# A retention layer and a SoLU block on one core: another written order of every engine's steps, with the loads of q, k and v placed one by one

## The chip, the cores and the metric

The kernel runs on one core of a Trainium2 chip. The metric is the device time of one execution in microseconds (us), as the median of several runs. The engines are called as the profile calls them: PE is TensorE (PEld its weight loads), DVE is VectorE, ACT is ScalarE, POOL is GpSimd, and SP is SyncE, whose queue issues nearly all DMA transfers.

## What is computed

```
# q, k, v: (8 batches, 8 heads, 576 tokens, 64), float32
scores = (q @ k.T) / 8
ret    = scores * gamma_h ** (row - col)   # 0 above the diagonal
x      = (ret @ v), heads side by side     # (4608 tokens, 512)
h      = x @ w_in                          # (4608, 1024)
solu   = h * softmax(h)
ln     = (solu - mean) / sqrt(var + 1e-6) * g_ln
out    = ln @ w_out                        # (4608, 512), float32
```

## The kernel before

The 4608 tokens are cut into 36 chunks of 128. Batches go in pairs: chunks 0, 2, 4, 6 are the first four pieces of batch 0, chunks 1, 3, 5, 7 those of batch 1, and chunk 8 holds the last 64 tokens of both; then the next pair begins. Retention is done in chunked form: within a chunk as masked scores times v, from earlier chunks through a state of 64 x 64 a head that each chunk passes on.

Nothing is scheduled by a tool. The string ORDER lists some 950 steps, `name:chunk:options`, and `run` (L826) calls them one after the other. Each engine gets its instructions in the order in which they are written there, and works them off in that order; between engines only semaphores order the work. So an instruction that waits holds up all that stands behind it on its engine. The steps of a chunk are:

- `ld` (L265): three transfers, q, k and v of the chunk, 256 KB each, on SP's queue. `li` (L778) loads one of four blocks of 128 rows of w_in, `lo` (L787) two of the eight blocks of w_out; each is 512 KB.
- `cq`, `ck`, `cv` (L285, L298, L310): q, k and v are scaled and cast to 16 bits, on POOL (`:g`), DVE (`:v`) or ACT (`:a`).
- `tq` and `eq` (L313, L363): PE transposes q and k (32 matmuls of 128 columns), and an engine copies the result to SBUF. In its place stand for some late chunks `tr`, `er` (L335, L344: q alone) and `kd` (L322: a DMA transpose of k).
- `sc` (L374) and `mk` (L387): the scores on PE, and two products with the mask on DVE.
- `kv` (L397), `ad` (L411), `dk` (L425), `d3` (L438): k.T v on PE, its addition to the state on DVE, and two decayed copies of the state on POOL.
- `av` (L449), `fs` (L463), `ex` (L482): x on PE from the scores and from the state; its cast to 16 bits.
- `m1` (L498): h, 16 matmuls of 512 columns. Chunks 0 and 1 do it with `mr` (L487), one row block of w_in at a time, each as soon as `wi` (L782) has cast it.
- `mx` (L508), `xp` (L515), `so` (L523): the row maximum on DVE, the exponential on ACT, the product h times exp on DVE, called u. h has two buffers in PSUM (`ps_h`, tag h): the matmuls of a chunk may begin when `so` of the chunk that held the buffer has ended.
- `ce` (L535): for the first five chunks (PLAIN = 5) the mean is taken from u, by two DVE instructions. For later ones the mean lies in w_out: `mm` (L809) multiplies w_out by ones, `mc` (L816) and `ws` (L820) subtract the mean from w_out.
- `sq` (L548), `ra` (L561), `rp` (L578): the sum of squares on ACT, two instructions on 128 x 1 on POOL or DVE, and their power on POOL.
- `tu` and `eu` (L584, L597), or `du` (L592): u transposed by PE (16 matmuls of 128 columns) and copied, or by a DMA transpose.
- `wo` (L792): a block of w_out is scaled and cast. `m2` (L602): the output product, 16 matmuls of 512 columns. `st` (L612): scaling on ACT, and the transfer to HBM.
- `wu` (L735): matmuls on zeros, which fill PE while it waits. The last chunk, 35, is done in halves of 512 columns (`hm` to `hw`, L628 to L717).

The strings BANKS and SLOTS say which PSUM bank and which buffer of a ring each tile takes. RINGS gives the depth of the rings, and is the same in both kernels.

## Time and profile before

| | |
|---|---|
| time, median of 3 runs | 211.8 us (211.57 to 212.08) |
| span of the profiled execution, first to last instruction | 210.9 us |
| PE, PEld busy | 92%, 59% |
| DVE, ACT, POOL busy | 86%, 81%, 75% |
| DMA moved | 47.71 MB, 226 GB/s on the mean |

The profile shows one execution. It has its span and no time of its own; the median of the runs stands 0.9 us above that span. In the rows of the trace the first number is the start in us from the span's start, the second the length; in brackets stands how long the engine was idle before, and what ended the idle time. In the rows by stage each engine has its busy time in the stage, and the number of its instructions.

### The profile page before, as it was taken

What the parts mean: (1) busy time and instruction counts of PE and PEld (TensorE: products, weight loads), DVE (VectorE), ACT (ScalarE), POOL (GpSimd) and SP (SyncE); (2) the same over time, 40 slices, a digit from 0 to 9 for tenths busy, and PEclk for the clock granted to TensorE, in tenths of its full rate; (3) what the DMA queues carried; (4) which work ended last, traced back from release to release, by engine and by line L of the source; (5) the groups of instructions that cost most, each with busy time, mean ns of one, the idle gap of its engine ahead of it and who ended that gap; (6) DMA issues with size and microseconds to landing.
All of it is one profiled execution on the core that took longest, in us unless ns stands there. A gap on an engine that the chain in (4) does not pass through costs nothing.

```text
span 210.9 us, 7583 instructions
## 1 busy us (share of the span) xinstructions
PE 194.3 (92%) x3125; PEld 124.0 (59%) x3125; DVE 181.4 (86%) x323; ACT 170.5 (81%) x299; POOL 157.2 (75%) x226
## 2 busy tenths in 40 slices
PE   0887798999999999999999999999999998999992
PEld 0464476575666657657566667575656654565562
DVE  0486999979997999899989999999879998999760
ACT  2424999898979999999898978999679976677981
POOL 5377899676689899888839798879999977545620
PEclk9999999999999999999999999999999999999999
DMA  5999998999898989999999899999989999899754
GB/s 134 257 330 294 258 272 290 253 209 299 224 215 258 265 215 273 221 251 230 208 275 197 205 231 238 273 226 206 179 143 256 210 166 205 156 247 199 154 174 149
DMA packets 110834, 47.71 MB, mean 226 GB/s; under 512 B 94536, under 2 KB 104784, under 8 KB 110800
## 3 DMA queue, kind: packets, MB, share of 16 engines
q1 hardware_dynamic: 110480, 47.07, 99.7%
q8 instruction: 24, 0.39, 0.8%
q10 hardware_dynamic: 320, 0.16, 0.3%
...
## 4 chain that ended last, share of the span: by engine, by line
PE 55%; SPq 14%; DMA 8%; DVE 8%; POOL 7%; ACT 3%; issue 3%; DVEq 0%; POOLq 0%
PE o L256 21%; PE h L256 18%; SPq L274 5%; SPq L270 5%; DMA w_out<-in_moe_w_out_dram 3%; PE tp L251 3%; PE sc L381 3%; PE lp L251 3%; DMA qkT<-k 2%; PE x L456 2%; POOL v L279 2%; SPq L789 2%; DMA qf<-in_q_dram 2%; PE x L256 2%; SPq L779 2%
## 5 line engine op out<-in xcount | busy, mean ns | idle before, releaser
L256 PE MATMUL h<-w_in,xT 128*64 128x512 f16 x560 | 66.9, 380 | 0.1
L256 PE MATMUL o<-w_c,uT 128*64 128x512 f16 x480 | 56.9, 380 | 0.0
L394 DVE TENSOR_TENSOR ret<-sc,tris 128x512 f16<-128x512 f32 x72 | 46.1, 682 | 2.8 <-PE sc L381 2.5
L256 PEld LDWEIGHTS <-xT 128*64 128x64 f16 x576 | 31.5, 110 | 23.1 <-issue 0.7
L512 DVE TENSOR_REDUCE nm<-h 128x1 f32<-128x1024 f32 x35 | 42.6, 1216 | 2.8 <-PE h L256 2.7
L256 PEld LDWEIGHTS <-uT 128*64 128x64 f16 x560 | 31.0, 110 | 23.0 <-issue 0.6
L527 DVE SCALAR_TENSOR_TENSOR u<-h,e 128x1024 f16<-128x1024 f32 x35 | 42.5, 1215 | 1.5 <-ACT e L518 1.4
L518 ACT ACTIVATE e<-h,nm 128x1024 f32<-128x1024 f32 x35 | 39.4, 1125 | 5.0 <-DVE nm L512 3.1
L432 POOL TENSOR_TENSOR s<-t,small 128x512 f16<-128x512 f32 x32 | 33.9, 1063 | 7.4 <-DVE t L420 6.1
L555 ACT ACTIVATE sq<-u,su 128x1024 bf16<-128x1024 f16 x30 | 34.8, 1159 | 2.0 <-DVE u L527 2.0
L581 POOL TENSOR_TENSOR rs<-w,mhalf 128x1 f32<-128x1 f32 x36 | 20.3, 570 | 20.7 <-DVE w L572 17.2
L290 POOL TENSOR_TENSOR q<-qf,small 128x512 f16<-128x512 f32 x30 | 31.2, 1043 | 5.4 <-DMA qf<-in_q_dram 5.1
L279 POOL TENSOR_TENSOR v<-vf,small 128x512 f16<-128x512 f32 x30 | 31.7, 1062 | 2.8 <-DMA vf<-in_v_dram 2.5
L615 ACT ACTIVATE o_sb<-o,rs 128x512 f32<-128x512 f32 x35 | 24.0, 692 | 4.5 <-POOL rs L581 3.2
L243 ACT COPY qkT<-tp 128x512 f16<-128x512 f16 x42 | 23.0, 599 | 5.0 <-PE tp L251 4.9
L243 ACT CAST xT<-x 128x512 f16<-128x512 f32 x29 | 17.1, 593 | 3.1 <-PE x L256 2.8
L251 PE MATMUL tp<-ident,q 128*64 128x128 f16 x232 | 12.4, 230 | 6.0 <-POOL q L290 5.5
L243 ACT CAST k<-kf 128x512 f16<-128x512 f32 x17 | 10.5, 626 | 7.7 <-DMA kf<-in_k_dram 7.7
L456 PE MATMUL x<-ret,v 128*64 128x128 f16 x288 | 14.8, 222 | 2.1 <-DVE ret L394 1.5
L251 PEld LDWEIGHTS <-q 128*64 128x64 f16 x280 | 11.0, 115 | 8.9 <-POOL q L290 5.7
L381 PE MATMUL sc<-qkT 64*128 64x128 f16 x288 | 14.7, 223 | 1.3 <-DMA qkT<-k 0.8
L444 POOL TENSOR_TENSOR s<-t,small 128x256 f32<-128x256 f32 x24 | 15.3, 638 | 0.9 <-DVE t L420 0.8
...
## 6 DMA issues: line engine op xcount, KB each, us to landing
...
uT<-u SPq DMA_TRANSPOSE x16, 4.6
...
```

The source lines that it names most:

```text
L243: (engine.copy if engine is nc.scalar else engine.tensor_copy)(out=out, in_=in_)
L251: nc.tensor.transpose(out=out[w], in_=in_[:, w], identity=ident)
L256: nc.tensor.matmul(out=out[w], lhsT=lhsT[:, w], rhs=rhs, start=start, stop=stop, skip_group_check=True,)
L279: engine.tensor_tensor(out=dst, in0=T.pop((key, n)), in1=table.unsqueeze(2).to_broadcast([P, H, D]), op=ALU.mult,)
L290: ENG[e].tensor_tensor(out=dst.rearrange("p (a h) d -> p h a d", h=2), in0=T.pop(("qf", n)).rearrange("p (h a) d -> p h a d", h=2), in1=ta ...
L394: nc.vector.tensor_tensor(out=r, in0=s, in1=m, op=ALU.mult)
L432: nc.gpsimd.tensor_tensor(out=s16, in0=t.unsqueeze(2).to_broadcast([P, 4, 2, D]), in1=gd.unsqueeze(3).to_broadcast([P, 4, 2, D]), op=ALU.mult,
L512: nc.vector.tensor_reduce(out=nm, in_=T["h", n], axis=AX.X, op=ALU.max, negate=True)
L518: nc.scalar.activation(out=e, in_=T["h", n], func=ACT.Exp, bias=T.pop(("nm", n)), accum_out=s)
L527: nc.vector.scalar_tensor_tensor(out=u, in0=T.pop(("h", n)), scalar=-1.0, in1=T.pop(("e", n)), op0=ALU.mult, op1=ALU.mult, accum_out=su,)
L555: nc.scalar.activation(out=s, in_=T.pop(("v", n)), func=ACT.Square, scale=-float(DFF), bias=T.pop(("su", n)), accum_out=ss,)
L615: nc.scalar.activation(out=o_sb, in_=T.pop(("o", n)), func=ACT.Copy, scale=T.pop(("rs", n)))
```

## The change

ORDER, BANKS and SLOTS are written anew. `ld` is taken apart into `lq`, `lk` and `lv`, so that each of the three transfers of a chunk has its own place in the order. The helper `both` makes the transposed tile of q and k where the first of its two halves needs it. The rules BY_DMA and BY_PE, which turned `tr`, `er` and `kd` of some chunks into `tq`, `eq` or nothing, are gone: the order names the step itself.

What the engines do in all stays nearly the same. PE has 32 transposes of u fewer (17 chunks by `tu`, 18 by `du`; 19 and 16 before) and 8 matmuls on zeros fewer (12, before 20). Of the pairs of `ra` 30 are on POOL (19 before) and 6 on DVE (17). `cv` is on DVE ten times (six), on POOL 26 times (30); `wo` is on POOL five times (three). SP issues two DMA transposes more. All else is a matter of order.

```diff
-BY_DMA = 12
-BY_PE = (12, 13, 14, 15, 16, 18, 19, 20, 21, 22, 23, 24, 25, 27)
 ORDER = """
-c1:0 ld:1 ld:0 cq:1:g cv:1:v ck:1:a cq:0:g tq:1 eq:1:av wu:2:2 wu:5:2 ck:0:a cv:0:g sc:1 ld:2 mk:1
...
+c1:0 lv:1 li:3 lk:1 lq:2 lq:1 ck:1:a lk:2 cv:1:v lq:0 wu:4:1 lq:4 cq:2:g gt:0 lk:0 li:0 ck:2:a
...
-    def ld(n):
-
-        for key, src in (("qf", q), ("kf", k), ("vf", v)):
-            dst = ring(load, [P, H, D], FP, key)
...
-            T[key, n] = dst
+    def load_one(n, key, src):
+        dst = ring(load, [P, H, D], FP, key)
+        if key == "qf" and quads(n) or key == "kf" and chunks[n][1] == 4:
+            nc.sync.dma_start(
+                out=dst.rearrange("p (h a) d -> p h (a d)", h=2), in_=fours(src, n)
+            )
+        else:
+            nc.sync.dma_start(out=dst, in_=tokens(src, n))
+        T[key, n] = dst
+
+    def lq(n):
+        load_one(n, "qf", q)
+
+    def lk(n):
+        load_one(n, "kf", k)
+
+    def lv(n):
+        load_one(n, "vf", v)
...
+    def both(n):
+
+        if ("qkT", n) not in T:
+            T["qkT", n] = ring(att, [P, 2, 4, P], F16, "qkT")
+        return T["qkT", n]
+
     def kd(n):
-        if chunks[n][1] == 4 or n < BY_DMA or n in BY_PE:
-            return
-        T["qkT", n] = ring(att, [P, 2, 4, P], F16, "qkT")
+
         nc.sync.dma_start_transpose(
-            out=T["qkT", n][:, 1], in_=T["k16", n].rearrange("p h d -> p (h d)")
+            out=both(n)[:, 1], in_=T["k16", n].rearrange("p h d -> p (h d)")
         )
...
     def tr(n):
-        if chunks[n][1] == 4 or n < BY_DMA or n in BY_PE:
-            return tq(n)
+
         tp = bank([P, 4, P], F16, "tr")
...
     def er(n, e="a"):
-        if chunks[n][1] == 4 or n < BY_DMA or n in BY_PE:
-            return eq(n, e)
-        turned(ENG[e], n, T["qkT", n][:, 0], T.pop(("tp", n)))
+        turned(ENG[e], n, both(n)[:, 0], T.pop(("tp", n)))
```

Three places show how the engines' orders differ. The first is the start of SP's queue. Before, q, k and v of chunk 1 are its first three transfers; the rows show what follows (qf, kf and vf are the loads of q, k and v: of chunk 0, of chunk 2, then the four blocks of w_in, then chunk 4).

```order
L270 DMA qf_118<-in_q_dram 128x2x256
L274 DMA kf_120<-in_k_dram 128x8x64
L274 DMA vf_122<-in_v_dram 128x8x64
L270 DMA qf_176<-in_q_dram 128x2x256
L274 DMA kf_178<-in_k_dram 128x8x64
L274 DMA vf_180<-in_v_dram 128x8x64
L779 DMA w_in32_94<-in_moe_w_in_dram 128x1024 x4
L270 DMA qf_371<-in_q_dram 128x2x256
L274 DMA kf_373<-in_k_dram 128x8x64
L274 DMA vf_375<-in_v_dram 128x8x64
```

SP's queue now, from its ninth transfer on (k of chunk 0, block 0 of w_in, v of 0, block 2, k of 4, block 1, v of 4, v of 2). Ahead of these rows stand v of 1, block 3 of w_in, k of 1, q of 2, q of 1, k of 2, q of 0 and q of 4.

```order
L275 DMA kf_138<-in_k_dram 128x8x64
L790 DMA w_in32_94<-in_moe_w_in_dram 128x1024
L275 DMA vf_176<-in_v_dram 128x8x64
L790 DMA w_in32_94<-in_moe_w_in_dram 128x1024
L275 DMA kf_196<-in_k_dram 128x8x64
L790 DMA w_in32_94<-in_moe_w_in_dram 128x1024
L275 DMA vf_212<-in_v_dram 128x8x64
L275 DMA vf_221<-in_v_dram 128x8x64
```

The last block of w_in was the 13th transfer, behind nine loads; it is the 14th now, behind ten, though the first block has moved up to the second place. v of chunk 4 was the 16th transfer and is the 15th, and v of chunk 2 was the ninth and is the 16th.

The second place is DVE's queue where the first h are done. Before (h_364 is that of chunk 1, h_379 of chunk 0, h_511 of chunk 2; nm is the maximum, u the product with the exponential):

```order
L512 TENSOR_REDUCE nm_405<-h_364 128x1
L512 TENSOR_REDUCE nm_420<-h_379 128x1
L527 SCALAR_TENSOR_TENSOR u_445,su_446<-h_364,e_415 128x1024
L420 TENSOR_TENSOR t_457<-kp_448,s32_362 128x256
L538 TENSOR_SCALAR nmu_462<-su_446 128x1
L543 TENSOR_SCALAR u_445<-u_445,nmu_462 128x1024
L394 TENSOR_TENSOR ret0_475<-sc0_465,tris_86 128x512
L394 TENSOR_TENSOR ret1_477<-sc1_466,tris_86 128x512
L527 SCALAR_TENSOR_TENSOR u_531,su_532<-h_379,e_508 128x1024
L420 TENSOR_TENSOR t_607<-kp_534,s32_384 128x256
L512 TENSOR_REDUCE nm_627<-h_511 128x1
```

And now (h_299 is that of chunk 1, h_398 of chunk 0, h_523 of chunk 2; t_428 is the state after chunk 2, ret0_450 and ret1_452 are the masked scores of chunk 4). Right ahead of these rows stands the cast of v of chunk 4 (`v16_391<-vf_212`, L289).

```order
L523 TENSOR_REDUCE nm_393<-h_299 128x1
L431 TENSOR_TENSOR t_428<-kp_416,s32_361 128x256
L405 TENSOR_TENSOR ret0_450<-sc0_434,tris_86 128x512
L405 TENSOR_TENSOR ret1_452<-sc1_435,tris_86 128x512
L538 SCALAR_TENSOR_TENSOR u_484,su_485<-h_299,e_395 128x1024
L431 TENSOR_TENSOR t_489<-kp_407,s32_430 128x256
L549 TENSOR_SCALAR nmu_513<-su_485 128x1
L554 TENSOR_SCALAR u_484<-u_484,nmu_513 128x1024
L523 TENSOR_REDUCE nm_542<-h_398 128x1
L523 TENSOR_REDUCE nm_575<-h_523 128x1
L431 TENSOR_TENSOR t_590<-kp_579,s32_426 128x256
L538 SCALAR_TENSOR_TENSOR u_609,su_610<-h_398,e_592 128x1024
```

A cast of v stands ahead of the first maximum; the state of chunk 2 and the masked scores of chunk 4 have moved ahead of the first u; and the maximum of chunk 2 has moved ahead of the u of chunk 0.

The third place is POOL's queue where w_out is cast. Before (w_out16 is the cast block, s32 a decayed state, rs the power of `rp`, w1 and w2 the two of `ra`):

```order
L279 TENSOR_TENSOR v16_766<-vf_656,small_85 128x512
L444 TENSOR_TENSOR s32_771<-t_457,small_85 128x256
L804 TENSOR_TENSOR w_out16_97<-w_out32_95,g32_93 128x512
L444 TENSOR_TENSOR s32_823<-t_607,small_85 128x256
L804 TENSOR_TENSOR w_out16_97<-w_out32_95,g32_93 128x512
L581 TENSOR_TENSOR rs_884<-w2_620,mhalf_88 128x1
L804 TENSOR_TENSOR w_out16_97<-w_out32_95,g32_93 128x512
```

Now:

```order
L443 TENSOR_TENSOR s16_588<-t_489,small_85 128x512
L443 TENSOR_TENSOR s16_595<-t_174,small_85 128x512
L455 TENSOR_TENSOR s32_597<-t_590,small_85 128x256
L443 TENSOR_TENSOR s16_599<-t_590,small_85 128x512
L289 TENSOR_TENSOR v16_622<-vf_278,small_85 128x512
L815 TENSOR_TENSOR w_out16_97<-w_out32_95,g32_93 128x512 x5
L577 TENSOR_SCALAR w1_685<-s_396 128x1
```

Three casts with other work between them have become five in a row, behind the states of chunks 3 and 4 and the v of chunk 6.

177 lines of the change are left out of this document (88 added, 89 removed).

## The prediction

> **What bounds the kernel now.** I read the page's busy shares first, then the busy time by stage, then the timeline of the first 45 us, in which the order has changed most.
>
> ```profile
> span 210.9 us, 7583 instructions
> ...
> PE 194.3 (92%) x3125; PEld 124.0 (59%) x3125; DVE 181.4 (86%) x323; ACT 170.5 (81%) x299; POOL 157.2 (75%) x226
> ```
>
> ```profile
> core 0: us, PE busy (x) PEld busy (x) DVE busy (x) ACT busy (x) POOL busy (x), PEclk, DMA share, GB/s
> 0.00:25.00 25.00, 15.71 (x221) 10.10 (x223) 14.09 (x28) 10.83 (x18) 16.01 (x28) 1.00 1.00 255
> 25.00:30.00 5.00, 5.00 (x100) 3.42 (x100) 4.96 (x10) 4.33 (x10) 4.58 (x7) 1.00 1.07 271
> 30.00:40.00 10.00, 9.32 (x175) 6.38 (x171) 9.79 (x18) 8.80 (x15) 9.61 (x12) 1.00 1.01 274
> ...
> 60.00:80.00 20.00, 20.00 (x350) 12.72 (x348) 17.94 (x31) 18.27 (x32) 18.39 (x26) 1.00 0.95 241
> 100.00:120.00 20.00, 19.52 (x308) 12.04 (x306) 18.46 (x33) 17.75 (x31) 14.28 (x20) 1.00 1.01 223
> 140.00:160.00 20.00, 19.24 (x322) 12.36 (x317) 18.23 (x31) 16.57 (x32) 18.25 (x28) 1.00 1.02 195
> 160.00:180.00 20.00, 19.18 (x310) 11.64 (x308) 18.41 (x33) 16.58 (x30) 17.09 (x23) 1.00 1.16 202
> ```
>
> Two regimes are to be seen. From 60 us on PE is busy in 20.00 of 20.00 us, or lacks 0.48 (100 to 120), 0.76 (140 to 160) and 0.82 (160 to 180), 2.1 us in all: there the end comes when PE's work is through, and a step moved costs something only if PE waits for it. In the first 25 us PE works 15.7, and between 25 and 40 us it is DVE that is full, 4.96 of 5 and 9.79 of 10, with POOL at 9.61 of 10. There the transfers set when work can begin, and DVE's queue sets how fast it goes on. PE cannot make up later what it loses there, since later it is full. So the time after is the time before, plus what the head loses, minus the work that PE no longer has, plus or minus the waits in the middle.
>
> **The pace of the transfers.** Instructions that waited for a transfer tell when it landed; here the first, the ninth, the 13th (the last block of w_in) and the 16th of SP's queue.
>
> ```profile
> 4.41 1.04 POOL L290 TENSOR_TENSOR q<-qf,small 128x512 f16<-128x512 f32 x1 [1.21 <-DMA qf<-in_q_dram]
> ...
> 13.52 1.04 POOL L279 TENSOR_TENSOR v<-vf,small 128x512 f16<-128x512 f32 x1 [0.29 <-DMA vf<-in_v_dram]
> ...
> 19.27 0.43 DVE L243 CAST w_in<-w_in 128x512 f16<-128x512 f32 x1 [0.98 <-DMA w_in<-in_moe_w_in_dram]
> ...
> 22.22 1.04 POOL L279 TENSOR_TENSOR v<-vf,small 128x512 f16<-128x512 f32 x1 [0.45 <-DMA vf<-in_v_dram]
> ```
>
> Eight loads took 9.11 us, 1.14 each; four blocks of w_in 5.75, 1.44 each; the next three loads 2.95, 0.98 each. With 1.14 and 1.44 the last block of w_in, now the 14th transfer behind nine loads and three blocks after the first, lands at 4.41 + 9 x 1.14 + 4 x 1.44 = 20.4 (before 19.27), v of chunk 4 at 21.6, v of chunk 2 at 22.7. With 0.98 a load all three come 1.4 to 1.8 us sooner. The early block of w_in gains nothing by itself: h of chunk 1 needs all four.
>
> **Term 1, DVE's chain in the head.** These rows show the chain before.
>
> ```profile
> 20.66 2.52 DVE L512 TENSOR_REDUCE nm<-h 128x1 f32<-128x1024 f32 x2 [0.96 <-PE h L256]
> ...
> 23.16 1.23 DVE L527 SCALAR_TENSOR_TENSOR u<-h,e 128x1024 f16<-128x1024 f32 x1
> ...
> 23.31 0.32 PE L405 MATMUL kp<-v,k 128*64 128x64 f16 x8 [0.95 <-POOL v L279]
> ...
> 24.20 0.61 POOL L243 CAST k<-kf 128x512 f16<-128x512 f32 x1
> ...
> 25.11 1.89 PE L256 MATMUL h<-w_in,xT 128*64 128x512 f16 x16
> ...
> 25.22 1.28 DVE L394 TENSOR_TENSOR ret<-sc,tris 128x512 f16<-128x512 f32 x2
> ...
> 26.42 1.21 DVE L527 SCALAR_TENSOR_TENSOR u<-h,e 128x1024 f16<-128x1024 f32 x1
> ...
> 28.73 1.49 PE L256 MATMUL h<-w_in,xT 128*64 128x512 f16 x12
> ```
>
> ```profile
> 37.40 1.92 PE L256 MATMUL h<-w_in,xT 128*64 128x512 f16 x16
> ...
> 38.60 1.03 POOL L804 TENSOR_TENSOR w_out<-w_out,g 128x512 f16<-128x512 f32 x1
> ...
> 40.52 3.21 PE L256 MATMUL o<-w_out,uT 128*64 128x512 f16 x28 [0.32 <-ACT w_out L797]
> ...
> 48.73 0.41 PE L251 MATMUL tp<-ident,k 128*64 128x128 f16 x8 [0.42 <-DVE k L243]
> ```
>
> ```profile
> L432 POOL TENSOR_TENSOR s<-t,small 128x512 f16<-128x512 f32 x32 | 33.9, 1063 | 7.4 <-DVE t L420 6.1 <-DVE t L418 0.9
> L279 POOL TENSOR_TENSOR v<-vf,small 128x512 f16<-128x512 f32 x30 | 31.7, 1062 | 2.8 <-DMA vf<-in_v_dram 2.5
> ...
> L420 DVE TENSOR_TENSOR t<-kp,s 128x256 f32<-128x256 f32 x24 | 10.0, 419 | 2.0 <-PE kp L405 1.3 <-POOL s L444 0.5
> ...
> L243 DVE COPY qkT<-tp 128x512 f16<-128x512 f16 x16 | 8.7, 567 | 0.4 <-ACT qkT L243 0.3
> ...
> L279 DVE TENSOR_TENSOR v<-vf,small 128x512 f16<-128x512 f32 x6 | 4.1, 690 | 6.1 <-DMA vf<-in_v_dram 6.1
> ...
> L444 POOL TENSOR_TENSOR s<-t,small 128x256 f32<-128x256 f32 x24 | 15.3, 638 | 0.9 <-DVE t L420 0.8
> ...
> L804 POOL TENSOR_TENSOR w_out<-w_out,g 128x512 f16<-128x512 f32 x3 | 3.3, 1096 | 0.0
> L543 DVE TENSOR_SCALAR u<-u,nmu 128x1024 f16<-128x1024 f16 x5 | 3.1, 613 | 0.2
> ...
> L538 DVE TENSOR_SCALAR nmu<-su 128x1 f32<-128x1 f32 x5 | 0.7, 146 | 0.0
> ```
>
> A maximum takes 1.26 (half of 2.52), u 1.21, a pair of masked scores 1.28, a state 0.42, the two of `ce` 0.76. Both h buffers are full from here on, so the h matmuls of chunk 2 wait for u of chunk 1 (ended 24.4, matmuls at 25.11) and those of chunk 4 for u of chunk 0 (ended 27.6, matmuls at 28.73). In the new order:
>
> - The first maximum stands behind the cast of v of chunk 4: 21.6 + 0.69 = 22.3, though h is done at about 21.4. It ends at 23.6.
> - Next in DVE's queue is the state of chunk 2, which needs that chunk's v: landed at 22.7, cast on POOL until 23.8, its products on PE (0.32) done at 24.1: 24.1 to 24.5. Then the masked scores of chunk 4 until 25.8, and only then u of chunk 1, until **27.0**. The matmuls of chunk 2 begin 2.0 us later than before and end at 29.0.
> - State and `ce` until 28.2, the maximum of chunk 0 until 29.5, and then the maximum of chunk 2, which was behind u of chunk 0, until 30.7; state, 31.1; u of chunk 0 until **32.3**. The matmuls of chunk 4 begin at 32.4, **3.7** later than at 28.73. ACT's exponentials run beside this and are there in time.
> - From there DVE does masked scores of 3, `ce`, u of 2, masked scores of 5, the maximum of 4, `ce`, one copy, a state and u of 4: 1.28 + 0.76 + 1.21 + 1.28 + 1.26 + 0.76 + 0.57 + 0.42 + 1.21 = 8.8, until 41.1. The matmuls of chunk 5 stood at 37.40; they come at 41.1, again 3.7 later. They take 1.9, and 0.9 of small PE steps lead to the product with ones (now ahead of all output products), which ends at 45.6.
>
> Before, PE had the same amount behind it at 42.3: twelve of the 28 products of the row at 40.52 (1.3 us), and the 16 small matmuls of x of chunk 6 that now stand ahead (0.45, as 16 transposes take below). That is a lag of 3.3. Some of it comes back at once, since before PE waited at 48.73 with 0.4 to 0.7 us of idle for a cast of k that now has more time: 2.9. With the quicker pace of 0.98 a load the chain begins 1.6 us sooner and the lag is 1.3. I take **2.4**, nearer the pace of 1.14, as that is from the stretch in which the same mixture of loads came.
>
> POOL gives the second bound. Behind the cast of v of chunk 2 (23.8) come two states of 0.64, the second of which waits for DVE until 24.5 (so 25.1), then ten operations of 1.04 to 1.06, two of 0.64 and one of 0.61 (12.4), and then the five casts of w_out in a row, 5 x 1.10. The last ends at about 43.0, and PE's product with ones just behind it, at 43.3, against 42.3 before. So even if DVE is on time the lag is **1.0**; with the pace of 0.98 here too, 1.8 sooner, it is nothing. On the other side I take 4 us, the 3.7 and a little. What is queued behind the waiting casts (`ra` and `rp` of chunk 1, q of chunks 10 and 7) is needed by PE about 43.5 to 46, and just fits.
>
> **Term 2, PE's work.** Two chunks' u are transposed by DMA and no longer by PE. A chunk's 16 transposes take this long:
>
> ```profile
> 51.32 0.45 PE lp L251 x16
> ```
>
> That is **-0.9**. The eight matmuls on zeros fewer stood in waits and count as nothing. What covers the two DMA transposes is other chunks' PE work between each and its use; without it each would cost up to the 5.15 us that a late k took before (below). The 22 small `ra` instructions that go from DVE to POOL lie beside PE's full stretches; they are nothing as long as POOL is not the one waited for.
>
> **Term 3, the middle.** The 2.1 us that PE lacks from 60 us on come in part from late transfers, as these pieces of the chain of waits show.
>
> ```profile
> 136.34 4.56 DMA qf<-in_q_dram
> ...
> 173.57 5.15 DMA qkT<-k
> ```
>
> The new order puts loads earlier ahead of their use in some places and later in others. I can name none that decides; all 2.1 us may go, and as many may come. I take nothing. The tail has the same steps with one output product more behind the last transposes, and one copy of the last chunk behind the rescaling factor; PE has work in both, so nothing.
>
> The sum against the span is 210.9 + 2.4 - 0.9 = 212.4, and with the 0.9 us by which the median of the runs stands above the span **213.3**.
>
> [...] The same transposes ran slower at the start, though the rows by stage give PE's clock as 1.00 there:
>
> ```profile
> 9.46 0.64 PE L251 MATMUL tp<-ident,k 128*64 128x128 f16 x8
> ...
> 21.95 0.42 PE L251 MATMUL tp<-ident,k 128*64 128x128 f16 x8
> ```
>
> [...]
>
> **The rivals.** *The middle pays for it (faster).* Place: the three stages between 100 and 180 us in which PE lacks 2.1 us. If the loads that are now placed one by one end all those waits, the gain is 2.1. For it speaks that two of the longest pieces of the chain there are transfers; against it, that as many new waits can come, and that the lag ahead of it is the larger. With a lag of 1.7, midway between POOL's bound and my 2.4: 211.8 + 1.7 - 0.9 - 2.1 = **210.5**. It decides from a lag of less than 3.0 minus what new waits cost. *It cancels (the same).* The lag is 0.9 to 1.0, POOL's bound, and equals the transposes removed: **211.8**. For it speaks the quick pace at 22 us. *POOL becomes the one waited for (slower still).* It gets two casts of w_out more, 2.2 us, just where it was busy 9.61 of 10, and the casts of q and k for chunks 7 to 10 stand behind them. If PE waits for these too, the price is 2.2 more: **215.5**. Against it: by the working above what stands behind them just fits. *The early block of w_in brings the head forward* would be the change doing what it says; the rows of SP's queue exclude it, as the last block comes later.
>
> **How the numbers follow.** Chances: the forecast 55%, with 212.2 to 214.9 as its own range (lag 1.3 to 4.0); the middle pays 21%; it cancels 11%; POOL 13%. The range reaches to the faster and the POOL case: 210.4 to 215.7. About 0.2% (0.4 us) is what a measurement of this kernel can tell from no change. Faster by more than that: 21%. The same: the 11% and a little of the forecast's edge, 12%. Slower: 67%.
>
> **What would show it.** In the profile after: the first maximum at about 22.3 (before 20.66); u of chunk 1 behind the masked scores of chunk 4, ended near 27.0; h of chunk 4 near 32.4, and PE idle ahead of it; the last cast of w_out on POOL near 43; the first output product behind 45. If h of chunk 4 begins before 30 us, term 1 is wrong. If PE lacks much more or less than 2.1 us between 60 and 200 us, term 3 is.

## The result, and the profile after

| | changed kernel | kernel before |
|---|---|---|
| time, median of 4 runs | 214.43 us (213.93 to 215.19) | 211.69 us (210.99 to 212.08) |
| ratio | 1.0118, 95% interval 1.0074 to 1.0163 | |
| profiled execution | 214.64 us, span 212.7 us | span 210.9 us |

The kernel became slower by 2.7 us; 1.5 had been forecast (213.3 against 211.8), with a range that holds the time. The terms of the sum did not come out as forecast, though: two large ones, of opposite sign, were not in it.

The page of the changed kernel begins so:

```profile
span 212.7 us, 7525 instructions
...
PE 193.9 (91%) x3085; PEld 121.7 (57%) x3085; DVE 182.6 (86%) x303; ACT 169.1 (80%) x295; POOL 163.9 (77%) x248
```

Here is the busy time by stage of the changed kernel, with the columns of the prediction's table:

```profile
core 0: us, PE busy (x) PEld busy (x) DVE busy (x) ACT busy (x) POOL busy (x), PEclk, DMA share, GB/s
0.00:25.00 25.00, 14.66 (x203) 9.04 (x203) 14.14 (x26) 11.08 (x18) 11.61 (x24) 1.00 1.03 258
25.00:30.00 5.00, 4.26 (x84) 3.13 (x82) 4.96 (x9) 3.94 (x9) 5.00 (x7) 1.00 1.16 257
30.00:40.00 10.00, 8.74 (x171) 6.35 (x168) 9.93 (x19) 9.80 (x18) 10.00 (x11) 1.00 1.02 323
40.00:50.00 10.00, 9.99 (x134) 5.89 (x132) 9.93 (x18) 9.07 (x16) 9.67 (x16) 1.00 1.12 221
53.00:62.00 9.00, 6.78 (x109) 4.65 (x104) 8.47 (x13) 3.87 (x7) 8.83 (x13) 0.81 0.95 238
65.00:200.00 135.00, 134.78 (x2208) 83.72 (x2206) 125.07 (x203) 118.75 (x209) 110.94 (x167) 1.00 1.02 219
100.00:120.00 20.00, 20.00 (x358) 13.04 (x354) 18.63 (x31) 19.12 (x34) 15.70 (x24) 1.00 0.92 229
140.00:160.00 20.00, 20.00 (x330) 12.39 (x328) 19.07 (x33) 18.90 (x35) 17.33 (x27) 1.00 1.14 208
160.00:180.00 20.00, 20.00 (x298) 11.54 (x296) 17.94 (x29) 16.68 (x31) 19.44 (x29) 1.00 1.23 202
```

Three rows of the kernel before that the prediction had no need of stand beside it:

```profile
40.00:50.00 10.00, 9.25 (x124) 6.21 (x123) 8.66 (x20) 9.39 (x18) 5.01 (x8) 1.00 1.02 246
53.00:62.00 9.00, 9.00 (x164) 5.82 (x162) 8.96 (x17) 7.81 (x13) 6.29 (x10) 1.00 0.97 233
65.00:200.00 135.00, 132.95 (x2172) 83.70 (x2170) 126.25 (x215) 117.73 (x208) 108.32 (x153) 1.00 1.05 218
```

Up to 40 us PE does a little less than before. From 53 to 62 us, where it was busy 9.00 of 9, it is busy 6.78, and at a mean clock of 0.81. And from 65 to 200 us, where it lacked 2.05 us, it lacks 0.22. POOL, half idle from 40 to 50 us before, is full there.

**A ledger of work.** Busy time hides slow matmuls (from 57 to 58 us of the changed kernel PE is busy 1.00 of 1 at a clock of 0.50) and counts those on zeros. So I add up, for all matmuls that began before a given time, what each takes when nothing holds it up, zeros left out. This row of the changed kernel's chain of waits gives 1.73 / 16 = 0.108 us for 512 columns; transposes take 0.45 / 16 = 0.028 us, as in the prediction, and scores 0.33 / 8 = 0.041 by a row of the same chain. The products of 64 columns are put at 0.027, an estimate: in the kernel before the 16 of x at 58.92 us hold PE for 0.42, 0.026 each. With 0.028 for all, or with the 0.015 that a row of the same chain gives for k.T v (0.12 / 8), no lag in this table would change by more than 0.1.

```profile
100.23 1.73 PE h L259 x16
```

| PE's work done, us | by 50 us | by 65 us | by 205 us | in all |
|---|---|---|---|---|
| before | 30.6 | 45.7 | 181.7 | 183.4 |
| changed | 29.5 | 40.3 | 179.0 | 182.5 |
| lag | 1.1 | 5.4 | 2.6 | -0.9 |

The lags come from sums that are not rounded. Against 183.4 and 182.5 in all, 1.7 and 3.5 us are left at 205 us: the changed kernel ends 1.8 later, which is the difference of the two spans. So the head loses 1.1; the stage from 50 to 65 us loses another **4.3**; the middle wins **2.8** back; and 0.9 is less work.

**The head** went as the prediction told it. The timeline of the changed kernel:

```profile
21.26 1.22 DVE L523 TENSOR_REDUCE nm<-h 128x1 f32<-128x1024 f32 x1
23.16 0.42 DVE L431 TENSOR_TENSOR t<-kp,s 128x256 f32<-128x256 f32 x1 [0.67 <-PE kp L416]
23.50 1.28 DVE L405 TENSOR_TENSOR ret<-sc,tris 128x512 f16<-128x512 f32 x2
24.69 1.22 DVE L538 SCALAR_TENSOR_TENSOR u<-h,e 128x1024 f16<-128x1024 f32 x1
25.97 1.92 PE L259 MATMUL h<-w_in,xT 128*64 128x512 f16 x16
29.63 1.21 DVE L538 SCALAR_TENSOR_TENSOR u<-h,e 128x1024 f16<-128x1024 f32 x1
30.90 1.92 PE L259 MATMUL h<-w_in,xT 128*64 128x512 f16 x16 [0.19 <-DVE u L538]
39.48 1.92 PE L259 MATMUL h<-w_in,xT 128*64 128x512 f16 x16 [0.38 <-DVE u L538]
```

State, masked scores, u, then h of chunk 2: the same chain as forecast, but 1.0 to 1.5 us sooner, since the loads came faster (the casts of v of chunks 4 and 2 began at 20.58 and 21.64, forecast 21.6 and 22.7; first maximum 21.26, forecast 22.3; u of chunk 1 ended 25.9, forecast 27.0; h of chunk 4 at 30.90, forecast 32.4). PE waits for u ahead of h of chunks 4 and 5.

**The stage from 53 us** was not foreseen. DVE's queue and PE's in the changed kernel:

```profile
52.47 1.09 DVE L289 TENSOR_TENSOR v<-vf,small 128x512 f16<-128x512 f32 x1
53.49 1.09 DVE L300 TENSOR_TENSOR q<-qf,small 128x512 f16<-128x512 f32 x1
54.50 1.26 DVE L832 TENSOR_TENSOR w_c<-w_out,warm 128x512 f16<-128x512 f16 x1
55.68 0.41 DVE L431 TENSOR_TENSOR t<-kp,s 128x256 f32<-128x256 f32 x1
...
56.15 0.32 PE L416 MATMUL kp<-v,k 128*64 128x64 f16 x8 [2.22 <-DVE t L431]
...
56.95 3.37 PE L259 MATMUL h<-w_in,xT 128*64 128x512 f16 x16
...
60.80 0.69 DVE L246 COPY qkT<-tp 128x512 f16<-128x512 f16 x1 [0.53 <-PE tp L254]
```

The products kv of chunk 9 need the PSUM bank that kv of chunk 7 took; that is free once DVE has added it to the state (`t`, at 55.68), and this step stands behind a cast of v, a cast of q and a subtraction of w_c. PE waits 2.22 us. Behind the wait its clock is halved: one-microsecond rows give 0.73, 0.50, 0.50 and 0.57 from 56 to 60 us, so (0.27 + 0.50 + 0.50 + 0.43) / 0.5 = 3.4 us at half rate. The 16 matmuls of h take 3.37 us there and 1.92 elsewhere, and DVE waits 0.53 us for the transposes behind them.

### The profile page after: what moved, and what is told of

It reads as the page before. It is cut to its first block, busy times and chain, and to the rows that moved or that the text cites. A ratio compares the mean times of both kernels' runs of the same rounds, so it can differ in the third digit from the quotient of the medians.

```text
span 212.7 us, 7525 instructions
## 1 busy us (share of the span) xinstructions
PE 193.9 (91%) x3085; PEld 121.7 (57%) x3085; DVE 182.6 (86%) x303; ACT 169.1 (80%) x295; POOL 163.9 (77%) x248
## 4 chain that ended last, share of the span: by engine, by line
PE 62%; POOL 11%; DVE 10%; SPq 6%; DMA 5%; issue 2%; ACT 1%; ACTq 0%; DVEq 0%; POOLq 0%
PE o L259 23%; PE h L259 19%; PE tp L254 4%; PE sc L392 4%; DMA vf<-in_v_dram 3%; PE lp L254 3%; DVE u L538 3%; POOL v L289 3%; SPq L790 3%; PE x L467 2%; DMA qkT<-q 2%; PE x L259 2%; POOL s L443 2%; DVE ret L405 2%; SPq L271 2%
## 5 line engine op out<-in xcount | busy, mean ns | idle before, releaser
L259 PE MATMUL h<-w_in,xT 128*64 128x512 f16 x560 | 69.3, 389 | 0.6 <-DVE u L538 0.6
L259 PEld LDWEIGHTS <-xT 128*64 128x64 f16 x576 | 32.0, 112 | 24.6 <-issue 2.4
L529 ACT ACTIVATE e<-h,nm 128x1024 f32<-128x1024 f32 x35 | 39.2, 1122 | 8.2 <-DVE nm L523 8.1
L259 PEld LDWEIGHTS <-uT 128*64 128x64 f16 x560 | 29.9, 110 | 23.5
L443 POOL TENSOR_TENSOR s<-t,small 128x512 f16<-128x512 f32 x32 | 34.4, 1078 | 6.3 <-DVE t L431 3.8
L300 POOL TENSOR_TENSOR q<-qf,small 128x512 f16<-128x512 f32 x31 | 32.3, 1049 | 7.9 <-DMA qf<-in_q_dram 7.6
L289 POOL TENSOR_TENSOR v<-vf,small 128x512 f16<-128x512 f32 x26 | 27.0, 1042 | 4.6 <-DMA vf<-in_v_dram 4.4
L246 ACT COPY qkT<-tp 128x512 f16<-128x512 f16 x40 | 21.8, 594 | 10.1 <-DVE qkT L246 6.3
L416 PE MATMUL kp<-v,k 128*64 128x64 f16 x256 | 9.7, 200 | 6.9 <-ACT k L246 4.2
L246 ACT CAST k<-kf 128x512 f16<-128x512 f32 x15 | 9.3, 618 | 7.5 <-DMA kf<-in_k_dram 7.5
L392 PEld LDWEIGHTS <-qkT 64*128 64x128 f16 x288 | 8.6, 97 | 11.3 <-issue 7.5
```

Of the source, the lines that this page charges most:

```text
L246: (engine.copy if engine is nc.scalar else engine.tensor_copy)(out=out, in_=in_)
L259: nc.tensor.matmul(out=out[w], lhsT=lhsT[:, w], rhs=rhs, start=start, stop=stop, skip_group_check=True,)
L289: engine.tensor_tensor(out=dst, in0=T.pop((key, n)), in1=table.unsqueeze(2).to_broadcast([P, H, D]), op=ALU.mult,)
L300: ENG[e].tensor_tensor(out=dst.rearrange("p (a h) d -> p h a d", h=2), in0=T.pop(("qf", n)).rearrange("p (h a) d -> p h a d", h=2), in1=ta ...
L392: nc.tensor.matmul(out=s[e][:, hp], lhsT=qkT[dd, 1, hp], rhs=qkT[dd, 0, hp], start=True, stop=True,)
L443: nc.gpsimd.tensor_tensor(out=s16, in0=t.unsqueeze(2).to_broadcast([P, 4, 2, D]), in1=gd.unsqueeze(3).to_broadcast([P, 4, 2, D]), op=ALU.mult,
```

## The experiments

Each ratio is to the kernel before, run on the same chip in between.

**The stage from 53 us: one step, the clock, or the whole queue?** First the state alone.

```diff
-ws:0:v ra:3:g st:0 mx:6 ws:2:v cv:9:v tu:3 cq:8:v cv:10:g lv:12 lq:15 lk:13 ws:1:v ex:7:a lv:13
-tq:9 rp:4 ad:7 st:2 eu:3:a lk:11 lq:14 kv:9 ws:6:v lv:17 sq:5 tq:8 ws:3:v cv:8:v ad:9 m1:7 dk:7
+ws:0:v ra:3:g st:0 mx:6 ws:2:v cv:9:v ad:7 tu:3 cq:8:v cv:10:g lv:12 lq:15 lk:13 ws:1:v ex:7:a lv:13
+tq:9 rp:4 st:2 eu:3:a lk:11 lq:14 kv:9 ws:6:v lv:17 sq:5 tq:8 ws:3:v cv:8:v ad:9 m1:7 dk:7
```

> The changed kernel with one step moved: DVE's addition to the state of chunk 7 (`ad:7`) stands right behind the cast of v of chunk 9, ahead of the cast of q of chunk 8 and of a subtraction of w_c. Theory (the PSUM bank of kv:9 is that of kv:7, and is held until `ad:7`, which stands too late in DVE's queue): the 2.2 us in which PE waits at 53.9 us are gone, PE's clock stays full behind them, and the time falls by 2.2 + about 1, to 211.3 us (210.9 to 212.3). Rival 1 (DVE is simply behind there, so that the wait moves to the next product that needs DVE): 213.5 to 214.5, with a wait of 1 us or more for DVE between 54 and 60 us. Rival 2 (the half clock at 56.5 us has nothing to do with the wait): the wait goes and the half clock stays, 212.4.

Measured: 215.79 us (214.2 to 217.76), ratio 1.0156 (1.0108 to 1.0204). Nothing was won. PE's waits in this kernel:

```profile
56.21 0.41 PE L254 MATMUL tp<-ident,q 128*64 128x128 f16 x8 [0.89 <-DVE q L300]
60.75 0.40 PE L392 MATMUL sc<-qkT 64*128 64x128 f16 x8 [1.73 <-ACT qkT L246]
```

The wait for the state is gone, but the transposes of chunk 8 now wait for the cast of q, and its scores for the copies: rival 1, though the time is even above its 213.5 to 214.5. What is late is DVE's queue, not one step in it. Rival 2 is out, as the time did not fall to 212.4. The clock alone would not decide that: it is 1.00 from 53 to 62 us here, but it is so too in a second execution of the changed kernel, below, in which PE waits 1.52 us for the state.

Next, matmuls on zeros in the wait, and nothing moved (BANKS gets one number more).

```diff
-tq:9 rp:4 ad:7 st:2 eu:3:a lk:11 lq:14 kv:9 ws:6:v lv:17 sq:5 tq:8 ws:3:v cv:8:v ad:9 m1:7 dk:7
+tq:9 rp:4 ad:7 st:2 eu:3:a lk:11 lq:14 wu:9:9 kv:9 ws:6:v lv:17 sq:5 tq:8 ws:3:v cv:8:v ad:9 m1:7 dk:7
```

> The changed kernel with nine products on zeros (18 matmuls of 512 columns, about 2 us) on a free PSUM bank ahead of kv:9, where PE waits 2.2 us for DVE. Nothing else is moved, so kv:9 begins when it did, at 56.1 us, or up to 0.3 later. Theory (the half clock from 56.5 to 59.9 us follows from the idle stretch): PE's granted clock stays full, the 16 matmuls of h behind it take 1.9 us in place of 3.4, and the time falls by 0.7 to 1.5, to about 213.3 us. Rival (the clock falls for another reason, or the half clock costs nothing since DVE sets the pace there): 214.4, no change.

Measured: 214.57 us (214.09 to 215.43), ratio 1.0119 (1.0075 to 1.0162): no change, the rival. PE's clock stays 1.00 from 53 us to the end in the profiled execution; over the other five runs its mean is 0.989 to 0.996, so that a half clock may stand somewhere in them. The times show no price of the half clock, but the traces do. From the cast of v of chunk 9 to the masked scores of chunk 8 DVE takes 8.94 and 8.95 us in the two executions with a half clock behind the wait (the changed kernel, and the one with the block of w_in moved, below). It takes 8.31, 8.31 and 8.32 in three without (this one, the changed kernel again and the one without `ce`, both below). So the half clock holds DVE's queue up by 0.6 us, less than these times can tell, and the other 8.3 are DVE's own.

Then the queue itself. Three subtractions that nobody needs yet are taken out of it, alone and with the state moved too; beside them the changed kernel once more.

```diff
-ws:0:v ra:3:g st:0 mx:6 ws:2:v cv:9:v tu:3 cq:8:v cv:10:g lv:12 lq:15 lk:13 ws:1:v ex:7:a lv:13
-tq:9 rp:4 ad:7 st:2 eu:3:a lk:11 lq:14 kv:9 ws:6:v lv:17 sq:5 tq:8 ws:3:v cv:8:v ad:9 m1:7 dk:7
-eq:8:va tq:10 eq:9:v sc:8 eq:10:va mk:8 lk:20 m2:4 sc:9 rp:3 m2:3 xp:6 st:4 mx:7 av:8 d3:9 mk:9
+ws:0:v ra:3:g st:0 mx:6 ws:2:v cv:9:v tu:3 cq:8:v cv:10:g lv:12 lq:15 lk:13 ex:7:a lv:13
+tq:9 rp:4 ad:7 st:2 eu:3:a lk:11 lq:14 kv:9 lv:17 sq:5 tq:8 cv:8:v ad:9 m1:7 dk:7
+eq:8:va tq:10 eq:9:v sc:8 eq:10:va mk:8 ws:1:v ws:6:v ws:3:v lk:20 m2:4 sc:9 rp:3 m2:3 xp:6 st:4 mx:7 av:8 d3:9 mk:9
```

> The changed kernel itself once more, as the measure for the three kernels beside it. Its ratio to the kernel before should again be 1.007 to 1.016. In the executions of kernels with this same order in the head, h of chunk 4 began at 30.9, 30.9, 32.0 and 32.1 us, so the head should lie in that range again.

> The changed kernel with three of the eight subtractions that give w_c (`ws:1`, `ws:6`, `ws:3`, on DVE) moved from between the casts of v and q of chunks 8 and 9 to behind the masked scores of chunk 8; the first product with w_c comes later still. Theory (from 52.5 to 61.5 us DVE works without a gap at steps that PE waits for one after the other, and so sets the pace; the subtractions, 1.26 and 1.79 us there, are not needed yet): the masked scores of chunk 8 begin about 2.5 us sooner, at 59 us, PE's idle time between 53 and 62 us falls from 2.2 us plus the half clock to about 1 us, and the time falls by 2 to 3 us: ratio to before 0.998 to 1.003. Rival 1 (the lag comes from the head and is only seen here): no change, 1.012. Rival 2 (the subtractions are now too late for the first product with w_c): PE waits for DVE near 66 us, 1.005 to 1.012.

The second has, on top of that:

```diff
-ws:0:v ra:3:g st:0 mx:6 ws:2:v cv:9:v tu:3 cq:8:v cv:10:g lv:12 lq:15 lk:13 ex:7:a lv:13
-tq:9 rp:4 ad:7 st:2 eu:3:a lk:11 lq:14 kv:9 lv:17 sq:5 tq:8 cv:8:v ad:9 m1:7 dk:7
+ws:0:v ra:3:g st:0 mx:6 ws:2:v cv:9:v ad:7 tu:3 cq:8:v cv:10:g lv:12 lq:15 lk:13 ex:7:a lv:13
+tq:9 rp:4 st:2 eu:3:a lk:11 lq:14 kv:9 lv:17 sq:5 tq:8 cv:8:v ad:9 m1:7 dk:7
```

> The same with the addition to the state of chunk 7 behind the cast of v of chunk 9 as well, so that both steps that held PE up between 53 and 62 us are mended. Theory: the state no longer stands behind the cast of q, so PE's wait ahead of kv:9 falls to 0.5 us or less, and the time is 0.3 to 1.0 us below the kernel with w_c late alone: ratio to before 0.994 to 1.000. Rival (moving the state only moved the wait on when it was done alone, and does no more here): the same time as with w_c late alone.

Measured: the changed kernel again 214.93 us (214.57 to 216.37), ratio 1.0160 (1.0113 to 1.0207), with h of chunk 4 at 33.51 us, outside the range that was expected; w_c late 213.27 (212.75 to 215.69), 1.0082 (1.0045 to 1.0119); with the state early too 212.93 (211.7 to 214.28), **1.0044** (1.0006 to 1.0081). The stage from 53 to 62 us, first with w_c late alone, then with both:

```profile
53.00:62.00 9.00, 7.95 (x144) 5.21 (x142) 8.95 (x16) 6.73 (x12) 8.83 (x13) 1.00 1.10 255
```

```profile
53.00:62.00 9.00, 8.41 (x146) 5.25 (x144) 9.00 (x16) 6.42 (x11) 8.83 (x12) 1.00 1.13 264
```

PE is busy 7.95 and 8.41 us there, where the changed kernel has 6.78 and, in its second execution, 6.56. By the ledger the work from 50 to 65 us is 12.6 and 13.5 us, in place of 10.7 and 12.1. So DVE's queue set the pace there, and what is late in it matters more than which single step PE is seen to wait for: the state moved up was worth nothing alone. The gain is about 1.7 and 2.0 us by the medians, less than the 2 to 3 that theory gave to the first; the 0.3 between them lies within the intervals, and the second missed its 0.994 to 1.000. Part of the first gain is lost to a new wait: with w_c late alone PE waits 0.98 us for DVE's masked scores of chunk 9, which now stand behind the three subtractions. Rival 2 had looked for a wait near there, but for the product with w_c.

**The head: does DVE's queue set it?**

```diff
     def ce(n):
 
+        if n < 2:
+            T["u", n] = T["v", n] = T.pop(("u0", n))
+            return
         nmu = tiny.tile([P, 1], FP, name="nmu")
```

> The changed kernel without the two DVE instructions of `ce` for chunks 0 and 1: the mean is not taken from u there, so the output rows of these two chunks are not the reference's. That takes 1.7 us out of DVE's queue ahead of 32 us and nothing else. Theory (DVE's queue sets the pace from the first u, near 25 us, to the masked scores of chunk 8, near 61 us): h of chunk 4 begins 0.5 to 0.9 us sooner, h of chunk 5 about 1.7 us sooner, and the whole gain is still there at 65 us, so the time falls by 1.2 to 1.7 us: ratio to before 1.003 to 1.008. Rival (POOL, busy 10.00 of 10 us from 30 to 40, sets the pace as much): no more than 0.5 us, 1.010 to 1.012.

Measured: 215.1 us (213.76 to 218.78), ratio 1.0147 (1.0083 to 1.021). The interval holds the rival's 1.010 to 1.012 and lies just above theory's 1.003 to 1.008: **the time shows no gain**. In the profiled execution h of chunk 4 begins at 30.79 us and h of chunk 5 at 38.72 (39.48 to 42.26 in executions with the two instructions); PE has done 30.4 us of work by 50 us, 1.8 more than the mean of ten executions given below, and 41.5 by 65, where the changed kernel has 39.2 and 40.3. Then PE waits for the state of chunk 7 for longer than before:

```profile
55.73 0.32 PE L416 MATMUL kp<-v,k 128*64 128x64 f16 x8 [2.66 <-DVE t L431]
```

So the trace shows that DVE's queue paces the head, and that a part of what is won there is lost again at 53 us, where PE waits for DVE and not for POOL, the engine that the rival named; the time doesn't show what is left.

**The block of w_in.**

```diff
-c1:0 lv:1 li:3 lk:1 lq:2 lq:1 ck:1:a lk:2 cv:1:v lq:0 wu:4:1 lq:4 cq:2:g gt:0 lk:0 li:0 ck:2:a
+c1:0 lv:1 lk:1 lq:2 lq:1 ck:1:a lk:2 cv:1:v lq:0 wu:4:1 lq:4 cq:2:g gt:0 lk:0 li:3 li:0 ck:2:a
```

> The changed kernel with the first block of w_in (`li:3`) moved from the second place of SP's queue to right ahead of the second block; the seven loads of q and k ahead of it come about 1 us sooner each. Theory (the first h needs all four blocks, and the last keeps its place; DVE's chain in the head begins with it): the last block lands within 0.3 us of 19.7, the first maximum within 0.3 us of 21.3, and the time stays within 0.4 us of 214.4. Rival 1 (the early block holds up all the first loads for nothing): about 1 us faster, 213.4. Rival 2 (the early block does bring the head forward): 0.5 to 1.5 us slower, 215 to 216.

Measured: 214.91 us (213.84 to 216.29), ratio 1.0133 (1.0087 to 1.0179), between the two results of the changed kernel. Its first maximum begins at 21.30 (21.26), h of chunk 4 at 30.94 (30.90), and its work by 50 us is the same 29.5. As far as these times can tell, the early block neither helps nor harms.

**The middle: what has closed PE's gaps?** Before, the 2.05 us that PE lacked from 65 to 200 us were four waits, and only the last was for a transfer:

```profile
104.29 0.47 PE L456 MATMUL x<-ret,v 128*64 128x128 f16 x8 [0.47 <-POOL v L279]
...
142.52 0.41 PE L251 MATMUL tp<-ident,q 128*64 128x128 f16 x8 [0.46 <-DVE t L420]
...
155.78 0.41 PE L251 MATMUL tr<-ident,q 128*64 128x128 f16 x8 [0.30 <-ACT o_sb L615]
...
178.76 0.40 PE L381 MATMUL sc<-qkT 64*128 64x128 f16 x8 [0.82 <-DMA qkT<-k]
```

First from the side of before: that transfer put earlier there.

```diff
-er:31:a ck:33:g so:27 du:27 fs:29 ex:29:a av:30 fs:30 ex:30:a ld:34 m2:24 tu:26 rp:25 mx:28 kd:33
+er:31:a ck:33:g so:27 du:27 fs:29 ex:29:a av:30 fs:30 ex:30:a kd:33 ld:34 m2:24 tu:26 rp:25 mx:28
```

> The kernel before with one step moved: the DMA transpose of k of chunk 33 is issued ahead of the three loads of chunk 34 and no longer behind them, so about 3 us sooner (170.6 us in place of 173.6). Theory (part of what PE lacked between 100 and 180 us was late transfers, which a better place in SP's queue ends): PE's idle 0.8 us at 178 us goes and the time falls by 0.6 to 0.9, to about 210.9 us. Rival (the loads of chunk 34, now 1.7 us later, bring a new wait, or the wait is taken over by another transfer): no change, 211.7.

Measured: 212.6 us (210.79 to 214.48), ratio 1.0032 (0.9994 to 1.0069): no gain, the rival. The 0.82 us at 178 us are gone, and these waits have come in their place (from 65 to 200 us PE lacks 2.51 us):

```profile
182.76 0.40 PE L381 MATMUL sc<-qkT 64*128 64x128 f16 x8 [0.36 <-DMA qkT<-q]
191.04 1.92 PE L256 MATMUL o<-w_c,uT 128*64 128x512 f16 x16 [0.92 <-DMA uT<-u]
```

Then from the side of the new order, on the kernel with w_c late and the state early (1.0044). One kernel issues 34 loads of chunks 13 to 33 later (two of them here), one gives nine pairs of `ra` back to DVE (one here).

```diff
-eq:8:va tq:10 eq:9:v sc:8 eq:10:va mk:8 ws:1:v ws:6:v ws:3:v lk:20 m2:4 sc:9 rp:3 m2:3 xp:6 st:4 mx:7 av:8 d3:9 mk:9
-kv:10 ad:10 fs:8 xp:7 lq:13 ex:8:a m2:5 ck:15:a sc:10 so:7 st:3 sq:7 so:6 ra:5:g mk:10 sq:6
-av:10 mx:8 st:5 ex:10:a eu:7:a m1:9 cq:15:v tu:6 mx:9 rp:6 m2:7 xp:8 ck:11:v kv:11 tq:11 eu:6:v
+eq:8:va tq:10 eq:9:v sc:8 eq:10:va mk:8 ws:1:v ws:6:v ws:3:v m2:4 sc:9 rp:3 m2:3 xp:6 st:4 mx:7 av:8 d3:9 mk:9
+kv:10 ad:10 fs:8 xp:7 ex:8:a m2:5 lk:20 ck:15:a sc:10 so:7 st:3 sq:7 so:6 ra:5:g mk:10 sq:6
+av:10 mx:8 st:5 ex:10:a eu:7:a m1:9 lq:13 cq:15:v tu:6 mx:9 rp:6 m2:7 xp:8 ck:11:v kv:11 tq:11 eu:6:v
...
```

> The kernel with w_c late and the state of chunk 7 early, in which 34 loads of q and k behind 57 us (chunks 11 to 33) are issued about 5 us of PE work later each, in the same order among themselves. That takes their mean lead over the cast back to what it was before (13.5 us of PE work for q and 14.6 for k, in place of 18.4 and 19.2). Theory (the middle has become gapless since the loads are placed one by one with more lead): PE lacks 1.5 to 3 us between 65 and 200 us, as in the kernel before (2.05), in place of 0 to 0.9 in the runs of the new order, and the time rises by 1.5 to 2.5 us: ratio to before 1.011 to 1.016. Rival (the lead was more than enough, and the middle is gapless for another reason): PE lacks less than 1 us there, and the time stays at 1.004.

```diff
-cv:27:g rp:15 ck:22:v lv:26 ra:16:g st:15 av:19 lv:31 lk:30 st:14 sc:20 so:17 ex:19:a sq:17 m2:16
+cv:27:g rp:15 ck:22:v lv:26 ra:16:v st:15 av:19 lv:31 lk:30 st:14 sc:20 so:17 ex:19:a sq:17 m2:16
...
```

> The kernel with w_c late and the state of chunk 7 early, in which the pairs of `ra` of nine chunks (15, 16, 23, 26, 27, 28, 29, 31, 33) run on DVE, as before the change, in place of POOL; nothing is moved. Theory (the middle has become gapless since POOL's powers no longer wait for DVE: 5.8 us in place of 17.2): POOL waits for DVE's `ra` again, 5 us or more longer, PE lacks 0.5 us or more on top of the 0 to 0.9 between 65 and 200 us, and the time rises by 0.5 to 1.5 us: ratio to before 1.007 to 1.012. Rival (idle time of POOL costs nothing): no change, 1.004.

Measured: loads later 216.66 us (214.38 to 217.94), ratio **1.0169** (1.0098 to 1.0241); `ra` on DVE 220.05 us (218.31 to 220.97), ratio **1.0332** (1.0273 to 1.0391). The first came out as its theory had it; the second cost far more than its 1.007 to 1.012. With the loads later PE lacks 1.79 us from 65 to 200 us (0.72 in the kernel it is made from). That is 1.1 of the 2.7 us by which the two ratios differ; the profiled execution is the second fastest of its six, and the rest is not seen in it. PE's longest waits there (0.79 us, and 0.74 at 143 us) are for casts of v, which stand on POOL behind casts of q that wait for their load:

```profile
65.00:200.00 135.00, 133.21 (x2168) 82.21 (x2166) 123.29 (x200) 117.93 (x208) 111.09 (x167) 1.00 1.00 220
...
133.49 0.41 PE L467 MATMUL x<-ret,v 128*64 128x128 f16 x8 [0.79 <-POOL v L289]
...
POOL q L300 <- DMA qf<-in_q_dram: 3.3, 2, 1.9
```

With `ra` on DVE it lacks 4.77 (6.37 up to 205 us), and in the lists of waits (us in total, times, longest) POOL's power waits for DVE as it did in the kernel before. First this kernel, from 65 us on, then the changed one and the one before, from 60 us on:

```profile
65.00:200.00 135.00, 130.23 (x2132) 80.66 (x2126) 124.43 (x214) 116.08 (x205) 104.78 (x148) 1.00 1.02 217
...
POOL rs L592 <- DVE w L583: 16.9, 7, 5.8
...
201.60 0.64 PE L259 MATMUL x<-qkT,s 128*64 128x64 f16 x16 [3.42 <-POOL s L443]
```

```profile
POOL rs L592 <- DVE w L583: 5.4, 2, 4.8
```

```profile
POOL rs L581 <- DVE w L572: 16.8, 9, 3.8
```

More than half of the 6.37 us is one wait near the end: the decayed state that PE needs at 201.60 us is made on POOL, whose powers wait for DVE 16.9 us in all. None of the four waits of the kernel before was for a state made on POOL. That kernel had its order made for `ra` on DVE and lacked 2.05; here the order was made for POOL, so the 4.77 says that the two belong together, not that `ra` on POOL was worth as much in the change. The same holds for the loads: the two kernels show what the new order depends on, and not which part of the change closed which of the four gaps.

**A version that beats both?** On the same base, first two copies moved from DVE to ACT:

```diff
-eq:8:va tq:10 eq:9:v sc:8 eq:10:va mk:8 ws:1:v ws:6:v ws:3:v lk:20 m2:4 sc:9 rp:3 m2:3 xp:6 st:4 mx:7 av:8 d3:9 mk:9
+eq:8:va tq:10 eq:9:a sc:8 eq:10:va mk:8 ws:1:v ws:6:v ws:3:v lk:20 m2:4 sc:9 rp:3 m2:3 xp:6 st:4 mx:7 av:8 d3:9 mk:9
```

> The kernel with w_c late and the state of chunk 7 early, and the two copies of `eq:9` on ACT in place of DVE. In the changed kernel ACT is busy 3.87 of 9 us between 53 and 62, DVE without a gap. Theory (DVE's steps there still set the pace): 1.2 us less stand ahead of the masked scores of chunk 8, which begin 0.6 to 1.2 us sooner, and the time falls by 0.5 to 1.0 us: ratio to before 0.999 to 1.002. Rival (what is left of the lag comes from the head alone): the same as without this, 1.004.

Measured: 212.56 us (212.08 to 213.9), ratio **1.0010** (0.9979 to 1.0041). The ratio is where theory had it, but the interval overlaps that of 1.0044, and the trace doesn't confirm the gain. The masked scores of chunk 8 begin at 58.32 us (59.06 without, 61.41 in the changed kernel), but 0.4 of these 0.74 us were won in the head (h of chunk 4 at 31.12 and 31.52). PE waits 0.58 us for a copy on ACT, and the work from 50 to 65 us is 13.3 us, against 13.5 without. Then two repairs more:

```diff
-tq:9 rp:4 st:2 eu:3:a lk:11 lq:14 kv:9 lv:17 sq:5 tq:8 cv:8:v ad:9 m1:7 dk:7
-eq:8:va tq:10 eq:9:a sc:8 eq:10:va mk:8 ws:1:v ws:6:v ws:3:v lk:20 m2:4 sc:9 rp:3 m2:3 xp:6 st:4 mx:7 av:8 d3:9 mk:9
+tq:9 rp:4 st:2 eu:3:a lk:11 lq:14 kv:9 lv:17 sq:5 tq:8 ad:9 m1:7 dk:7
+eq:8:va tq:10 eq:9:a sc:8 eq:10:va mk:8 cv:8:v ws:1:v ws:6:v ws:3:v lk:20 m2:4 sc:9 rp:3 m2:3 xp:6 st:4 mx:7 av:8 d3:9 mk:9
...
-m1:29 sc:33 ex:31:a ra:27:g er:32:a sc:32 ck:34:v du:28 d3:32 m1:31 dk:31 mk:33 sq:26 cq:35:g
-kd:34 mx:29 sq:30 lv:34 kq:34 tq:35 mk:32 m2:27 eq:35:a xp:29 lv:35 d3:31 mx:31 rp:27 av:32 fs:32
+m1:29 sc:33 ex:31:a ra:27:g er:32:a sc:32 ck:34:v kq:34 kd:34 du:28 d3:32 m1:31 dk:31 mk:33 sq:26 cq:35:g
+mx:29 sq:30 lv:34 tq:35 mk:32 m2:27 eq:35:a xp:29 lv:35 d3:31 mx:31 rp:27 av:32 fs:32
```

> The kernel with w_c late, the state of chunk 7 early and the copies of `eq:9` on ACT, with two more repairs read from its trace: the cast of v of chunk 8 (1.53 us on DVE at 54.7 us) goes behind the masked scores of chunk 8, since its first use comes at 62.8 us; and the two DMA transposes of chunk 34, of q and of k, are issued ahead of that of u of chunk 28 and no longer behind it (PE waits 1.1 us for the one of q at 185.8 us; in the executions of the new order so far it lacked 0 to 1.1 us between 180 and 200). Theory (each is a wait that nothing else covers): PE lacks 0.6 to 0.9 us less between 53 and 62 us, and nothing at 185 us, and the time falls by 0.8 to 1.8 us: ratio to before 0.993 to 0.998, faster than both kernels. Rival (as when the state of chunk 7, or the transpose of k of chunk 33, was moved alone, the next instruction in the queue is late in its place): no change, 1.001.

Measured: 213.81 us (212.96 to 216.9), ratio 1.0087 (1.005 to 1.0124): the expectation failed. Both waits it aimed at are gone, and a new one stands behind them:

```profile
64.90 0.28 PE L416 MATMUL kp<-v,k 128*64 128x64 f16 x6 [1.59 <-DVE ret L405]
...
180.00:200.00 20.00, 19.91 (x270) 12.21 (x266) 17.89 (x28) 17.03 (x30) 11.21 (x24) 1.00 0.89 189
```

With the cast of v of chunk 8 and the three subtractions in a row, the masked scores of chunk 9 come late. This wait of 1.59 us is as long as the difference to 1.0010; why the two waits that are gone bring nothing was not followed. No version tried is faster than the kernel before; the best is level with it.

## Why the prediction was right or wrong

**Term 1, the head: right in mechanism, and of about the right size.** It put the lag at 2.4, with 0 to 4 as bounds. The profile shown with the result has 1.1. But the transfers differ from one execution to the next: in ten profiled executions of kernels whose order is the changed one's up to 50 us, h of chunk 4 begins between 30.9 and 33.5 us, and the work done by 50 us is 27.0 to 29.5, on the mean 28.6; two executions of the order before (one with the transpose of k of chunk 33 moved) have 30.6 and 30.2. So the lag is **1.9** on the mean, and in none did h of chunk 4 begin before the 30 us that the prediction named as its test. The kernel with zeros in the wait came nearly at the pace that was forecast (first maximum 22.3, u of chunk 1 ended 27.0, h of chunk 4 at 32.4):

```profile
22.39 1.22 DVE L523 TENSOR_REDUCE nm<-h 128x1 f32<-128x1024 f32 x1
25.83 1.22 DVE L538 SCALAR_TENSOR_TENSOR u<-h,e 128x1024 f16<-128x1024 f32 x1
32.03 1.92 PE L259 MATMUL h<-w_in,xT 128*64 128x512 f16 x16 [0.19 <-DVE u L538]
```

What varies is above all v of chunk 2, the 16th transfer, on which by the new order the first u hangs. The products with it waited 0.53 us in the first execution of the changed kernel and 2.29 in the second, in which h of chunk 4 began at 33.51:

```profile
22.73 0.32 PE L416 MATMUL kp<-v,k 128*64 128x64 f16 x8 [0.53 <-POOL v L289]
```

```profile
24.51 0.32 PE L416 MATMUL kp<-v,k 128*64 128x64 f16 x8 [2.29 <-POOL v L289]
...
33.51 1.92 PE L259 MATMUL h<-w_in,xT 128*64 128x512 f16 x16 [0.15 <-DVE u L538]
```

That the early block gains nothing was right (1.0133 without it).

**Term 2, the transposes: right.** The work is 182.5 in place of 183.4 us, and no long wait for the two new DMA transposes was seen: from 60 to 205 us the profile of the changed kernel lists one wait of PE for a DMA transpose, of 0.2 us.

**Term 3, the middle: this step failed, and twice.** "I take nothing" was to stand for gains and losses that cancel. In truth PE lacked far less than 2.1 us behind 65 us: the waits nearly all went, which the rival in which the middle pays had priced at 2.1. From 65 to 200 us it lacked 0.01 to 0.91 us in five executions with the changed order there, 0.5 on the mean, against 2.05 and 2.51 before. (From 60 us on, the stretch that the prediction named, the second execution lacked 1.68, of which 0.92 still belong to the stage before 65 us.) The work from 65 to 205 us is 138.1 to 138.8 in the five, against 136.0 and 135.4: **-2.8** on the mean, of which 1.8 are these waits and 1.0 lies in stretches in which PE is shown as busy. The new order needs the loads' lead and `ra` on POOL, as the two kernels that take them back show; what closed the gaps of the old one stays open. And a new wait came where PE had been full before, from 53 to 62 us: **+3.7** (work from 50 to 65 us 11.2 on the mean of three executions, 14.9 before; 10.7 in the two with the half clock there, 12.1 in the third). The prediction looked for new waits where before had old ones, and never worked through DVE's queue behind 45 us: there the subtractions of w_c and the casts for chunks 8 and 9 have come between the steps that PE waits for. POOL, the third rival, was as full as feared, 10.00 of 10 and 9.67 of 10, but PE was not seen waiting for its casts of w_out.

The sum of the four by the means is +1.9 - 0.9 - 2.8 + 3.7 = **+1.9** against a forecast of +1.5, so that the total came near was luck: two errors in one term nearly cancelled. The spans say the same: 212.7, 214.4 and 213.4 in the same three executions (the last with the block of w_in moved), 213.5 on the mean, against 210.9 and 212.2 before, 211.55. The medians are 2.7 apart; 0.2 of that lies outside the span (runs of the changed kernel stand 1.9 to 2.0 us above their spans, those of before 1.7, so the 0.9 of the prediction mixed two executions); the rest is within the spread of single executions.

**The slow matmuls at the start.** At the start the matmuls of the changed kernel were slow for longer than before, though the column of the clock gives 1.00: eight matmuls of scores took 0.60 us as late as 17.98 us, and 0.40 at 22.98; before, 0.61 at 11.75 us and 0.40 at 15.57. In the second execution of the changed kernel two matmuls of h took 0.38 at 18.67 us, as much as two products at 39.81 us before; in the first, eight took 1.23 at 18.51, where eight products take 1.05 with w_c late at 65.30. So this differs between executions. At the last row block of chunk 1's h PE was no longer slow: the twelve matmuls at 20.60 us took 1.48, as the twelve at 28.73 before took 1.49. What the slow start is worth in the lag of the head was not separated. Behind the wait of 2.22 us that ends at 56.15 us matmuls were slow again, and there the column shows it, with 0.50.
